# Block 0's x2 in an attention and two-MLP kernel: the last group's sum by ScalarE copies and accumulating transfers in place of VectorE adds

## The chip, the cores and the metric

The kernel runs on one core of a Trainium2 chip. The metric is the device time of one execution in microseconds (us); the median of three runs of the kernel before is 578.8 us (578.77 to 579.1). Engines are named as in the profile: PE (TensorE matmul), DVE (VectorE), ACT (ScalarE), POOL (GpSimd, which here mostly issues transfers) and SP (SyncE, which issues loads). Each engine works through its own instructions in the order in which they stand and waits for the others by semaphores.

## The reference

What is computed, cut to what matters:

```
x   = decayed linear attention of q, k, v       # batch 2, 768 steps, 8 heads of 64
xn  = x / sqrt(mean(x*x) + 1e-6) * rms_g        # 1536 tokens x 512
x2  = (silu(xn @ w_gate) * (xn @ w_val)) @ w_out   # 512 -> 1536 -> 512
h   = x2 @ w_in                                  # 512 -> 2048
out = max(0.01 * h, h) @ w_out2                  # 2048 -> 512
```

All of it is float32; the weights come as int64 bit patterns of float64 and are converted on the chip.

## The kernel before, in words

Tokens lie in three **blocks** of 512. The first MLP makes x2 from 12 slices f of 128 hidden features, in three **groups** of four (gi 0, 1, 2); the second MLP takes 16 slices in four groups (gi 3 to 6). Every float32 matmul operand is split into a **high** part (a rounded copy, by ACT) and a **low** part (the rest, by a DVE subtraction), and a product is three matmuls.

Blocks 1 and 2 are multiplied together with seven products instead of eight by `quad`: its steps p1 to p7 put half products into PSUM banks X, Y and Z. Three banks are read in mid-use: p1 fills X, ACT copies it (`kept_sum`, L1070, tile `is`), then p6 adds to X, ACT copies it again (tile `iu`), and only then may p7 add to X; DVE reads X (L1079) before p4 adds to it once more. So PE waits inside a quad for ACT's copies of bank X. Before p6 all pending entries of the list `sums` are emitted.

Block 0 is done by plain products (`whole`) and `down`. Its x2 of the three groups is summed thus: after group 0 ACT copies the four PSUM banks into the tile `more` (L752) and POOL writes them to four DRAM tiles `held` (L754); after group 1 the same with a transfer that adds in DRAM (L756); in group 2, each `down` fetches one `held` tile into a quarter of `more` (L729), and at the end `evac1` adds the four PSUM banks to the quarters with DVE (L750). After that the high parts `x2h` (ACT, L786) and low parts `x2l` (DVE, L789) of the four quarters are made; they are put on the list `sums`. The first product of the second MLP that needs them is `whole("i", f, 0)`.

The order of the work is set twice: `plan` lists PE's steps, `run` hands out conversion work and entries of `sums` between them by a planner's clocks (`spend`), and the scheduler of the tile framework then settles the place of each instruction on its engine.

Of the kernel before, what the change touches and what calls it, by code (L numbers as in the profile page):

```python
# [13 lines left out]
AF = mybir.ActivationFunctionType  # L14
ALU = mybir.AluOpType
# [6 lines left out]
G1 = [4, 4, 4]  # L22
# [4 lines left out]
SUMS = 2  # L27
# [38 lines left out]
def chain_kernel(ctx: ExitStack, tc: tile.TileContext, qk_t, kv, w1, w2, mask, qdec, kdec, sdec, rms_g, ident, out):  # L66
    nc = tc.nc
# [27 lines left out]
    held = [dram.tile([P, 512], F32, name=f"held{i}") for i in range(4)]  # L95
# [13 lines left out]
    def bank(name):  # L109
        return pools["ps"].tile([P, 512], F32, tag="bank", name=name)  # L110
# [296 lines left out]
    groups = [list(range(sum(g[:i]), sum(g[:i + 1]))) for g in (G1, G2) for i in range(len(g))]  # L407
    groups = [("gvo" if i < len(G1) else "ip", fs) for i, fs in enumerate(groups)]
# [231 lines left out]
    def need(key):  # L640
        while key not in wt:
            assert upcoming()
            convert_next()


    def product_t(dst, w, h, l, which=slice(0, 12)):

        parts = [slice(k * P, (k + 1) * P) for k in range(4)]
        pairs = [(w[:, i, part], h[:, k, :]) for k, part in enumerate(parts) for i in range(2)]
        pairs += [(w[:, 0, part], l[:, k, :] if l is not None else None) for k, part in enumerate(parts)]  # L650
        for n, (lhs, rhs) in list(enumerate(pairs))[which]:
            nc.tensor.matmul(  # L652
                out=dst, lhsT=lhs, rhs=rhs, start=(n == 0), stop=(n == len(pairs) - 1), skip_group_check=True
            )
# [5 lines left out]
    x2h, x2l = {}, {}  # L660

    sums = []
    made, parted = {}, {}
    pools = {}
    parts = {}
# [2 lines left out]
    def accumulate(L, g, f, b, start, stop, transposed):  # L668

        if start:  # L670
            acc["b"] = acc_banks(f"a{L}_{g}_{b}", 4)
        h, l = parted.pop((L, f, b))
        w = wt[f"{L}{f}"]
        for m in range(4):
            part = slice(m * P, (m + 1) * P)
            if transposed:
                terms = (w[:, 0, part], h), (w[:, 0, part], l), (w[:, 1, part], h)
            else:
                terms = (h[:, part], w[:, 0, :]), (h[:, part], w[:, 1, :]), (l[:, part], w[:, 0, :])
            cut = 256 if stop and m == 3 and g == len(groups) - 1 else 512  # L680
            for c in range(0, 512, cut):
                for n, (lhs, rhs) in enumerate(terms):
                    nc.tensor.matmul(  # L683
                        out=acc["b"][m][:, c:c + cut],
                        lhsT=lhs,
                        rhs=rhs[:, c:c + cut],
                        start=(start and n == 0),
                        stop=(stop and n == 2),
                        skip_group_check=True,
                    )  # L690
# [3 lines left out]
    def upper(key):  # L694
        if key in made:
            x = made.pop(key)
            h = gp.tile([P, 512], F32R, tag="gh", name="g{}_{}_{}h".format(*key))
            nc.scalar.activation(out=h, in_=x, func=AF.Copy)
            spend("a", 0.52)
            halves[key] = x, h  # L700

    def lower(key):
        if key in halves:
            x, h = halves.pop(key)
            l = gp.tile([P, 512], F32R, tag="gl", name="g{}_{}_{}l".format(*key))
            nc.vector.tensor_tensor(out=l, in0=x, in1=h.bitcast(F32), op=ALU.subtract)
            parted[key] = h, l
            spend("v", 0.6)
            if key[0] in "qr":
                follow(*key)  # L710
                spend("v", 0.6 if key[2] in (1, 3, 5, 6) else 0.0)
# [9 lines left out]
    def down(gi, f, b):  # L721
        kinds, fs = groups[gi]
        L = kinds[-1]
        key = (L, f, b)
        upper(key)
        lower(key)
        if gi == len(G1) - 1:
            m = f - fs[0]
            nc.gpsimd.dma_start(out=extra()[:, m, :], in_=held[m])  # L729
        accumulate(L, gi, f, b, f == fs[0], f == fs[-1], L == "o" or b > 0)  # L730
        used(f"{L}{f}")
        if f == fs[-1]:
            banks = acc.pop("b")
            first = gi in (0, len(G1))
            by_copy = gi in (0, len(G1)) or b == 0 and gi not in (len(G1) - 1, len(groups) - 1)
            later.append(("a" if by_copy else "v", 2.4, lambda: (evac1 if L == "o" else evac2)(gi, b, banks)))
        placed[0] = order.index(key) + 1

    def evac1(gi, b, banks):
        last = gi == len(G1) - 1  # L740
        if b:
            acc[b] = xp.tile([P, 4, 512], F32, tag=f"acc{b}", name=f"x2acc{b}")
            for m in range(4):
                nc.scalar.activation(out=acc[b][:, m, :], in_=banks[m], func=AF.Copy)
            return
        acc[0] = extra()
        for m in range(4):
            t = acc[0][:, m, :]
            if last:
                nc.vector.tensor_tensor(out=t, in0=banks[m], in1=t, op=ALU.add)  # L750
                continue
            nc.scalar.activation(out=t, in_=banks[m], func=AF.Copy)  # L752
            if gi == 0:
                nc.gpsimd.dma_start(out=held[m], in_=t)  # L754
            else:
                nc.gpsimd.dma_start(out=held[m], in_=t, accum_op=ALU.add)  # L756
        if last:
            high, low = x2_parts(0)
            sums.extend([lambda m=m, do=do: do(m) for do in (high, low) for m in range(4)])

    x2_ops = {}

# [17 lines left out]
    def x2_parts(b):  # L780
        if b not in x2h:
            x2h[b] = xp.tile([P, 4, 512], F32R, tag=f"xh{b}", name=f"x2h{b}")
            x2l[b] = xp.tile([P, 4, 512], F32R, tag=f"xl{b}", name=f"x2l{b}")

        def high(m):
            nc.scalar.activation(out=x2h[b][:, m, :], in_=acc[b][:, m, :], func=AF.Copy)  # L786

        def low(m):
            nc.vector.tensor_tensor(  # L789
                out=x2l[b][:, m, :], in0=acc[b][:, m, :], in1=x2h[b][:, m, :].bitcast(F32), op=ALU.subtract  # L790
            )

        return high, low
# [132 lines left out]
    def extra():  # L926
        if not more:
            more[0] = xp.tile([P, 4, 512], F32, tag="acc0", name="more")
        return more[0]
# [86 lines left out]
    def used(key):  # L1016

        n, f = key[0], int(key[1:])
        left[key] = left.get(key, 2 if doubled(n, f) else NB) - 1
        if not left[key]:  # L1020
            free(key)
# [15 lines left out]
    def consume_later(n, f, b):  # L1037
        later.append(("v" if n == "v" else "a", 0.62 if n == "v" else 0.52, lambda: consume(n, f, b)))

    def whole(n, f, b, h, l):  # L1040
        products[n, f, b] = x = bank(f"{n}{f}_{b}")
        product_t(x, wt[f"{n}{f}"], h[b], l[b])
        used(f"{n}{f}")
        consume_later(n, f, b)
# [190 lines left out]
    def pair(p):  # L1235
        return 2 * p, 2 * p + 1
# [30 lines left out]
    def do(token):  # L1267
        if token in alone:
            alone[token]()
        elif ":" in token:  # L1270
            convert_step(*token.split(":"))
        elif token[:2] in by_chunk:
            by_chunk[token[:2]](int(token[2:]))
        elif token[:2] in by_pair_of:
            by_pair_of[token[:2]](pair(int(token[2:])))
        elif token[0] == "T":
            terms.pop(token[1:])()
        else:
            n, f, b = token[1], int(token[2]), int(token[3])
            if token[0] in by_step:  # L1280
                by_step[token[0]](n, f, b)
            elif token[0] == "D":
                down(0, f, b)
            else:
                (upper if token[0] == "U" else lower)((n, f, b))
# [22 lines left out]
    def run(i, keys, b, step, behind):  # L1308
        need(keys[0])
        start = max(clock["pe"], done.get(keys[0], 0.0))  # L1310
        step()
        clock["pe"] = start + (1.36 if keys[-1] == "half" else 2.72)
        next_parts(upper)
        next_parts(lower)
        for _ in range(min(len(sums), SUMS)):
            sums.pop(0)()
            spend("v", 1.13)
            spend("a", 0.97)
        limit = clock["pe"] + (OVER if behind else 0.0)
        while upcoming():  # L1320
            key, engine, cost, _ = converting[0]
            if max(clock[engine], done.get(key, 0.0)) + cost > limit:
                break
            convert_next()
        flush()
# [73 lines left out]
```

## Time and profile before

| what | us |
|---|---|
| median of three runs | 578.8 |
| the profiled execution, its own time | 578.74 |
| its span | 576.8 |
| outside the span (578.74 - 576.8) | 1.94 |
| PE busy | 566.7 (98%) |
| DVE busy | 502.3 (87%) |
| ACT busy | 406.9 (71%) |
| POOL busy | 42.0 (7%) |

The last matmul begins at 571.84 us, and the span ends at 576.8. The place of the change lies between 315 and 345 us, where the first MLP ends and the second begins. All times within the execution are counted from the span's start.

### The profile page before, as it was taken

Reading aid. Unit: us, or ns where it says so; the run is one execution under the profiler, and the core shown is the slowest. Engines: PE = TensorE matmul, PEld = TensorE weight load, DVE = VectorE, ACT = ScalarE, POOL = GpSimd, SP = SyncE. Lnnn points to the kernel's source line nnn. Section 1 sums busy time; section 2 is a strip of 40 time slices with the busy share of each in tenths; the row PEclk is TensorE's granted clock in tenths of the full one; section 3 lists DMA queues with packets and bytes.
Section 4 is the critical chain, followed back from the end, with each engine's and each line's share of the span. In section 5 each row is a group of like instructions: output and inputs, shape, how many; then the busy total and the mean of one; then the engine's idle time right before and its main releaser. Section 6 shows DMA issues by size and latency. Waiting matters only on the chain.

```text
span 576.8 us, 8536 instructions
## 1 busy us (share of the span) xinstructions
PE 566.7 (98%) x3082; PEld 466.1 (81%) x3082; DVE 502.3 (87%) x986; ACT 406.9 (71%) x744; POOL 42.0 (7%) x49
## 2 busy tenths in 40 slices
PE   8999999999999999999999999999999999999996
PEld 5888788888888888888888878878888888888885
DVE  8899989985776899986899999999999989996792
ACT  4799768977656556977647589989868986676330
POOL 3341300010000000010000100000100020002100
PEclk9999999999999999999999999999999999999999
DMA  8991422442211122236220222224422252102455
GB/s 339 408 351 38 147 73 74 145 147 73 74 58 30 60 74 68 80 87 133 73 74 4 70 73 75 72 74 145 147 74 74 93 114 85 39 0 34 113 92 128
DMA packets 34202, 59.28 MB, mean 103 GB/s; under 512 B 19184, under 2 KB 19440, under 8 KB 34160
## 3 DMA queue, kind: packets, MB, share of 16 engines
q1 hardware_dynamic: 30864, 51.39, 26.8%
q0 software_dynamic: 3008, 7.34, 5.7%
q8 instruction: 24, 0.39, 0.3%
q14 instruction: 18, 0.15, 0.1%
q10 hardware_dynamic: 288, 0.01, 0.0%
HBM read 50.34 MB, written 8.39 MB: 102 GB/s over the span
## 4 chain that ended last, share of the span: by engine, by line
PE 87%; DVE 5%; DMA 5%; ACT 2%; issue 1%; POOL 0%; SPq 0%; DVEq 0%; POOLq 0%; ACTq 0%
PE X L853 11%; PE ao L683 9%; PE Z L853 9%; PE iX L1053 8%; PE i L652 8%; PE ap L683 7%; PE v L652 7%; PE g L652 6%; PE vX L1053 5%; PE gX L1053 5%; PE iZ L1053 4%; PE gZ L1053 2%; PE vZ L1053 2%; DMA qkv<-in_qk_t 2%; DMA qkv<-in_kv 2%; PE iY L1053 2%
## 5 line engine op out<-in xcount | busy, mean ns | idle before, releaser
L683 PE MATMUL ap<-w_p,gp_0h 128*128 128x512 f32 (+1 forms) x130 | 39.8, 386 | 0.0
L652 PE MATMUL i<-x2h,w_i 128*128 128x512 f32 x128 | 32.3, 389 | 0.0
L652 PE MATMUL g<-xh,w_g 128*128 128x512 f32 x128 | 31.8, 390 | 0.0
L652 PE MATMUL v<-xh,w_v 128*128 128x512 f32 x128 | 31.8, 390 | 0.0
L683 PE MATMUL ao<-go_0h,w_o 128*128 128x512 f32 x96 | 31.0, 389 | 0.0
L683 PEld LDWEIGHTS ap<-w_p,gp_0h 128*128 128x128 f32 x130 | 24.3, 188 | 5.0
L652 PEld LDWEIGHTS g<-xh,w_g 128*128 128x128 f32 x128 | 24.0, 188 | 5.1 <-issue 0.2
L652 PEld LDWEIGHTS i<-x2h,w_i 128*128 128x128 f32 x128 | 24.0, 188 | 5.0
L652 PEld LDWEIGHTS v<-xh,w_v 128*128 128x128 f32 x128 | 24.0, 188 | 5.0
L991 ACT ACTIVATE more<-i 128x512 f32<-128x512 f32 x16 | 9.6, 600 | 22.1 <-PE i L652 22.0
L683 PE MATMUL ap<-w_p,gp_0l 128*128 128x512 f32 (+1 forms) x65 | 25.1, 386 | 0.0
L1053 PE MATMUL iX<-th,w_si 128*128 128x512 f32 x64 | 20.7, 397 | 1.2 <-ACT iu L1070 0.7
L683 PEld LDWEIGHTS ao<-go_0h,w_o 128*128 128x128 f32 x96 | 18.0, 188 | 3.7
L1053 PE MATMUL iZ<-x2h,w_si 128*128 128x512 f32 x64 | 20.2, 391 | 0.0
L555 DVE TENSOR_TENSOR w_o<-wa_o,w_o 128x512 fp32r<-128x512 f32 x12 | 8.3, 688 | 12.5 <-ACT w_o L551 12.5
L683 PE MATMUL ao<-go_0l,w_o 128*128 128x512 f32 x48 | 18.7, 389 | 0.0
L652 PE MATMUL v<-xl,w_v 128*128 128x512 f32 x64 | 17.2, 391 | 0.0
L652 PE MATMUL g<-xl,w_g 128*128 128x512 f32 x64 | 17.2, 391 | 0.0
L884 DVE TENSOR_TENSOR y2acc<-X,y2acc 128x512 f32<-128x512 f32 x26 | 17.1, 686 | 0.2 <-PE X L853 0.2
L652 PE MATMUL i<-x2l,w_i 128*128 128x512 f32 x64 | 17.1, 389 | 0.0
L1053 PEld LDWEIGHTS iX<-th,w_si 128*128 128x128 f32 x64 | 11.8, 188 | 5.2 <-ACT iu L1070 1.4
L257 DVE TENSOR_TENSOR a<-sc,mask_sb 128x1024 f32<-128x1024 f32 (+1 forms) x13 | 14.5, 1137 | 1.1 <-PE sc L245 1.0
(372 smaller groups left out, 1824.9 us busy)
## 6 DMA issues: line engine op xcount, KB each, us to landing
raw_i<-in_w SPq DMA_DIRECT2D x16, 512.0 KB, 3.6
raw_p<-in_w SPq DMA_DIRECT2D x16, 512.0 KB, 3.6
raw_g<-in_w SPq DMA_DIRECT2D x12, 512.0 KB, 3.5
raw_v<-in_w SPq DMA_DIRECT2D x12, 512.0 KB, 3.5
raw_o<-in_w SPq DMA_DIRECT2D x12, 512.0 KB, 3.5
qkT<-in_qk_t SPq DMA_DIRECT2D x7, 512.0 KB, 8.4
kv<-in_kv SPq DMA_DIRECT2D x7, 512.0 KB, 9.2
out<-more POOLq DMA_DIRECT2D x12, 256.0 KB, 5.0
```

What stands on the lines that cost most here:

```text
L257: nc.vector.tensor_tensor(out=s["a"][:, j], in0=s["sc"][:, j], in1=mask_sb[:, j], op=ALU.mult)
L555: v.tensor_tensor(out=u[:, 1, :], in0=a, in1=u[:, 0, :].bitcast(F32), op=ALU.subtract)
L652: nc.tensor.matmul(out=dst, lhsT=lhs, rhs=rhs, start=(n == 0), stop=(n == len(pairs) - 1), skip_group_check=True)
L683: nc.tensor.matmul(out=acc["b"][m][:, c:c + cut], lhsT=lhs, rhs=rhs[:, c:c + cut], start=(start and n == 0), stop=(stop and n == 2), skip_ ...
L853: nc.tensor.matmul(out=acc[side][m], lhsT=lhs, rhs=rhs, start=(start and f == fs[0] and k == 0), stop=(f == fs[-2] and k == 2), skip_group ...
L884: nc.vector.tensor_tensor(out=dst, in0=banks[m], in1=dst, op=ALU.add)
L991: nc.scalar.activation(out=a, in_=x, func=AF.Prelu, alpha=0.01)
L1053: nc.tensor.matmul(out=dst, lhsT=lhs, rhs=rhs, start=(start and n == 0), stop=(n == 5), skip_group_check=True)
```

## The change

`evac1` no longer adds group 2's banks to a fetched sum by DVE. ACT copies each bank into its quarter of `more`, as it does for the other groups, and POOL then issues a transfer per quarter that adds the DRAM tile `held` into `more` in SBUF (`accum_op`). The four fetches in `down` go. The eight part-making operations of block 0 stand on a list of their own, `block0`; it is not emptied before p6 but when `sums` is empty or before the first `whole("i", ...)`. In the planner's clock the evacuation counts as ACT work (`by_copy`).

```diff
@@ down
         lower(key)
-        if gi == len(G1) - 1:
-            m = f - fs[0]
-            nc.gpsimd.dma_start(out=extra()[:, m, :], in_=held[m])
         accumulate(L, gi, f, b, f == fs[0], f == fs[-1], L == "o" or b > 0)
...
-            by_copy = gi in (0, len(G1)) or b == 0 and gi not in (len(G1) - 1, len(groups) - 1)
+            by_copy = gi in (0, len(G1)) or b == 0 and gi != len(groups) - 1
@@ evac1
             t = acc[0][:, m, :]
+            nc.scalar.activation(out=t, in_=banks[m], func=AF.Copy)
             if last:
-                nc.vector.tensor_tensor(out=t, in0=banks[m], in1=t, op=ALU.add)
-                continue
-            nc.scalar.activation(out=t, in_=banks[m], func=AF.Copy)
-            if gi == 0:
+                nc.gpsimd.dma_start(out=t, in_=held[m], accum_op=ALU.add)
+            elif gi == 0:
                 nc.gpsimd.dma_start(out=held[m], in_=t)
             else:
                 nc.gpsimd.dma_start(out=held[m], in_=t, accum_op=ALU.add)
         if last:
             high, low = x2_parts(0)
-            sums.extend([lambda m=m, do=do: do(m) for do in (high, low) for m in range(4)])
+            block0.extend([lambda m=m, do=do: do(m) for do in (high, low) for m in range(4)])
@@ whole
+        while n == "i" and block0:
+            block0.pop(0)()
@@ run
-        for _ in range(min(len(sums), SUMS)):
-            sums.pop(0)()
+        for _ in range(min(len(sums) + len(block0), SUMS)):
+            (sums or block0).pop(0)()
```

Three places show what the scheduler makes of it. On ACT, at the end of group 2, before: `x2h_3381<-more` are block 0's high parts, `is` and `iu` are the two copies of bank X (`iX_3396`) in the first quad of the second MLP, `wa_p` and `w_i` belong to weight conversion.

```order
L786 ACTIVATE x2h_3381<-more 128x512 [waits DVE_49] x4
L1070 ACTIVATE is_0_3407<-iX_3396 128x512 [waits PE_49]
L969 ACTIVATE th<-x2acc_1705 128x1024 [waits DVE_49]
L603 ACTIVATE wa_p_3492<-raw_p_3113 128x512 [waits DVE_49]
L991 ACTIVATE is_0_3407<-is_0_3407 128x512 [waits DVE_49]
L698 ACTIVATE gq_1h<-is_0_3407 128x512 [waits Activation_49]
L603 ACTIVATE wa_p_3534<-raw_p_3393 128x512 [waits DMAHW3_49,DVE_49]
L1070 ACTIVATE iu_0_3457<-iX_3396 128x512 [waits PE_49]
L1070 ACTIVATE is_0_3466<-iZ_3459 128x512
```

The same place on ACT in the changed kernel, from the second copy of a bank on:

```order
L747 ACTIVATE more<-ao_0_1_3305 128x512 [waits PE_49,Activation_49]
L603 ACTIVATE wa_p_3494<-raw_p_3113 128x512 [waits DVE_49]
L747 ACTIVATE more<-ao_0_2_3306 128x512 [waits PE_49,Activation_49]
L747 ACTIVATE more<-ao_0_3_3307 128x512 [waits PE_49,Activation_49]
L966 ACTIVATE th<-x2acc_1705 128x1024 [waits DVE_49]
L1069 ACTIVATE is_0_3407<-iX_3396 128x512 [waits PE_49]
L783 ACTIVATE x2h_3381<-more 128x512 [waits DMASW0_49]
L783 ACTIVATE x2h_3381<-more 128x512 [waits DMASW1_49]
L783 ACTIVATE x2h_3381<-more 128x512 [waits DMASW2_49]
L551 ACTIVATE w_i_3489<-wa_i_3433 128x512 [waits DVE_49]
L988 ACTIVATE is_0_3407<-is_0_3407 128x512 [waits DVE_49]
L783 ACTIVATE x2h_3381<-more 128x512 [waits DMASW3_49]
```

The next row there is `L1069 ACTIVATE iu_0_3451<-iX_3396 128x512 [waits PE_49]`, the second copy of bank X. The high parts now wait for the four transfers (DMASW0 to DMASW3), and the copy `iu` stands behind the fourth of them.

On PE, from the first quad's p5 on, before (`iZ_3459` is p5, `iX_3396<-th,w_si_3421` p6, `iX_3396<-th,w_si_3422` p7, `3506` and `3515` the next quad's banks):

```order
L1053 MATMUL iZ_3459<-x2h_3190,w_si_3422 128x512
L1053 MATMUL iZ_3459<-x2h_3190,w_si_3422 128x512 [waits DVE_49]
L1053 MATMUL iZ_3459<-x2l_3191,w_si_3422 128x512
L1053 MATMUL iZ_3459<-x2h_3190,w_si_3422 128x512 x2
L1053 MATMUL iZ_3459<-x2l_3191,w_si_3422 128x512
L1053 MATMUL iX_3506<-x2h_3256,w_i_3430 128x512
L1053 MATMUL iY_3515<-x2h_3256,w_i_3430 128x512 [waits DVE_49]
L1053 MATMUL iX_3396<-th,w_si_3421 128x512 [waits DVE_49]
L1053 MATMUL iX_3396<-tl,w_si_3421 128x512
L1053 MATMUL iX_3396<-th,w_si_3421 128x512 x2
L1053 MATMUL iX_3396<-tl,w_si_3421 128x512
L1053 MATMUL iX_3396<-th,w_si_3422 128x512 [waits Activation_49]
```

PE in the changed kernel, the rest of p6, p5, three matmuls of the next quad and p7's first:

```order
L1052 MATMUL iX_3396<-th,w_si_3421 128x512 [waits DVE_49]
L1052 MATMUL iX_3396<-tl,w_si_3421 128x512
L1052 MATMUL iX_3396<-th,w_si_3421 128x512 x2
L1052 MATMUL iX_3396<-tl,w_si_3421 128x512
L1052 MATMUL iZ_3453<-x2h_3190,w_si_3422 128x512 x2
L1052 MATMUL iZ_3453<-x2l_3191,w_si_3422 128x512
L1052 MATMUL iZ_3453<-x2h_3190,w_si_3422 128x512 x2
L1052 MATMUL iZ_3453<-x2l_3191,w_si_3422 128x512
L1052 MATMUL iX_3502<-x2h_3256,w_i_3430 128x512
L1052 MATMUL iX_3502<-x2h_3256,w_i_3430 128x512 [waits DVE_49]
L1052 MATMUL iX_3502<-x2l_3257,w_i_3430 128x512
L1052 MATMUL iX_3396<-th,w_si_3422 128x512 [waits Activation_49]
```

p6 now follows its first matmul at once and stands ahead of p5; p7 still waits for ACT. Since the quad begins, 26 matmuls stand ahead of p7 before the change and 27 after it.

On DVE, before, from the last low parts of block 2 on:

```order
L750 TENSOR_TENSOR more<-ao_0_0_3305,more 128x512 [waits DMASW0_49,PE_49]
L750 TENSOR_TENSOR more<-ao_0_1_3306,more 128x512 [waits DMASW1_49,PE_49]
L750 TENSOR_TENSOR more<-ao_0_2_3307,more 128x512 [waits DMASW2_49,PE_49]
L750 TENSOR_TENSOR more<-ao_0_3_3308,more 128x512 [waits DMASW3_49,PE_49]
L966 TENSOR_TENSOR x2acc_1705<-x2acc_1705,x2acc_1939 128x1024 [waits DVE_49]
L492 TENSOR_TENSOR w_si_3422<-wa_i_3108,w_si_3422 128x512
L1079 TENSOR_TENSOR is_0_3407<-iY_3409,is_0_3407 128x512 [waits PE_49,Activation_49]
L972 TENSOR_TENSOR tl<-x2acc_1705,th 128x1024 [waits Activation_49]
L492 TENSOR_TENSOR w_si_3421<-wa_i_3046,w_si_3421 128x512
L789 TENSOR_TENSOR x2l_3382<-more,x2h_3381 128x512 x4
```

The same place on DVE in the changed kernel:

```order
L492 TENSOR_TENSOR w_si_3422<-wa_i_3108,w_si_3422 128x512
L963 TENSOR_TENSOR x2acc_1705<-x2acc_1705,x2acc_1939 128x1024 [waits DVE_49]
L492 TENSOR_TENSOR w_si_3421<-wa_i_3046,w_si_3421 128x512
L555 TENSOR_TENSOR w_i_3430<-wa_i_3388,w_i_3430 128x512
L548 ISA wa_i_3433<-wa_i_3433,wb_i_3434 128x1024
L969 TENSOR_TENSOR tl<-x2acc_1705,th 128x1024 [waits Activation_49]
L1078 TENSOR_TENSOR is_0_3407<-iY_3409,is_0_3407 128x512 [waits PE_49,Activation_49]
L786 TENSOR_TENSOR x2l_3382<-more,x2h_3381 128x512 [waits DMASW0_49,Activation_49]
L786 TENSOR_TENSOR x2l_3382<-more,x2h_3381 128x512 [waits DMASW1_49,Activation_49]
L786 TENSOR_TENSOR x2l_3382<-more,x2h_3381 128x512 [waits DMASW2_49,Activation_49]
L786 TENSOR_TENSOR x2l_3382<-more,x2h_3381 128x512 [waits DMASW3_49,Activation_49]
```

The four adds are gone, the low parts of the weights (`w_si`) stand where they were, and the low parts of block 0 now wait for the transfers and for ACT. On POOL the four transfers keep their place among its instructions.

## Rows read from the trace of the kernel before

**Rows 1.** Stretches (us): each engine's busy time, its instructions, granted clock, DMA share.

```profile
core 0: us, PE busy (x) PEld busy (x) DVE busy (x) ACT busy (x) POOL busy (x), PEclk, DMA share, GB/s
329.00:338.00 9.00, 7.77 (x33) 5.83 (x32) 8.70 (x13) 7.43 (x12) 0.00 (x0) 1.00 0.18 58
338.00:572.00 234.00, 233.95 (x1031) 192.33 (x1030) 207.90 (x391) 168.44 (x298) 11.59 (x16) 1.00 0.30 82
```

**Rows 2.** Timeline of PE: start, us, instruction, idle before and its releaser.

```profile
327.43 0.61 PE L683 MATMUL ao<-go_0h,w_o 128*128 128x512 f32 x2
...
329.69 0.62 PE L1053 MATMUL iX<-x2h,w_i 128*128 128x512 f32 x2
...
332.41 0.39 PE L1053 MATMUL iX<-th,w_si 128*128 128x512 f32 x1
...
335.16 0.50 PE L1053 MATMUL iX<-th,w_si 128*128 128x512 f32 x1 [0.55 <-DVE w_si L492]
...
337.28 0.72 PE L1053 MATMUL iX<-th,w_si 128*128 128x512 f32 x2 [0.69 <-ACT iu L1070]
337.84 0.40 PE L1053 MATMUL iX<-tl,w_si 128*128 128x512 f32 x1
```

**Rows 3.** Timeline of DVE.

```profile
328.16 2.48 DVE L750 TENSOR_TENSOR more<-ao,more 128x512 f32<-128x512 f32 x4
330.56 1.22 DVE L966 TENSOR_TENSOR x2acc<-x2acc,x2acc 128x1024 f32<-128x1024 f32 x1
...
334.42 0.68 DVE L492 TENSOR_TENSOR w_si<-wa_i,w_si 128x512 fp32r<-128x512 f32 x1
```

**Rows 4.** Timeline of ACT.

```profile
314.42 1.14 ACT L786 ACTIVATE x2h<-x2acc 128x512 fp32r<-128x512 f32 x2
...
328.88 2.43 ACT L786 ACTIVATE x2h<-more 128x512 fp32r<-128x512 f32 x4 [4.75 <-DVE more L750]
...
331.81 1.06 ACT L969 ACTIVATE th<-x2acc 128x1024 fp32r<-128x1024 f32 x1
...
336.63 0.60 ACT L1070 ACTIVATE iu<-iX 128x512 f32<-128x512 f32 x1 [0.81 <-PE iX L1053]
...
468.09 0.60 ACT L918 ACTIVATE more<-ap 128x512 f32<-128x512 f32 x1 [0.18 <-PE ap L683]
```

**Rows 5.** One line: the plain fetch into SBUF, L729.

```profile
DMA to landing us min/median/max: 2.8/2.9/3.0
```

**Rows 6.** One line: the accumulating transfer of group 1, L756.

```profile
L756 POOL DMA_DIRECT2D held<-more x4: 904/1234/1430, 256.7 to 259.0; - x4
DMA to landing us min/median/max: 3.8/5.7/11.1
```

**Rows 7.** One line: the accumulating transfers of the second MLP, L922.

```profile
DMA to landing us min/median/max: 3.7/5.7/6.8
```

**Rows 8.** Timeline of POOL, in both stretches with L922.

```profile
468.99 3.65 POOL L922 DMA_DIRECT2D out<-more  x4 [56.43 <-ACT more L918]
...
471.48 1.15 POOL L922 DMA_DIRECT2D out<-more  x1
...
528.82 3.65 POOL L922 DMA_DIRECT2D out<-more  x4 [56.19 <-ACT more L918]
...
531.32 1.15 POOL L922 DMA_DIRECT2D out<-more  x1
```

**Rows 9.** DMA issues at 471.48 and at 528.82: KB, us to landing.

```profile
out<-more POOLq DMA_DIRECT2D x1, 256.0 KB, 6.1
...
out<-more POOLq DMA_DIRECT2D x1, 256.0 KB, 4.0
```

**Rows 10.** SP's timeline at 333 us, and DMA packets, 330 to 338 us.

```profile
333.45 0.33 SPq L454 DMA_DIRECT2D raw_p<-in_w  x1
...
q1 hardware_dynamic: 144, 0.52, 20.0%
```

More of the change, by code (lines that the diff above doesn't have):

```diff
@@ L662, in chain_kernel @@
     sums = []
+    block0 = []
     made, parted = {}, {}
```

## The prediction

> **What bounds the kernel now.** I read the busy times by stretch first. From 338 to 572 us PE is busy 233.95 of 234 us at a granted clock of 1.00, and from 329 to 338, where the changed instructions stand, 7.77 of 9.00 [rows 1]. So PE sets the end, and near the change it has 1.23 us of gaps; after them it has none. Whatever the change takes from or adds to PE's waits here comes through to the end unchanged, and work that it spares DVE or ACT is worth nothing by itself.
>
> PE's timeline gives the two gaps [rows 2]: 0.55 us before the matmul at 335.16, ended by DVE's low part of `w_si`, and 0.69 us before the one at 337.28, ended by ACT's second copy of bank X (`iu`). The first is p6 and the second p7 of the first quad. The gaps understate the loss, because a matmul's row is longer than its slot: from 329.69 to 332.41 PE issued 12 matmuls, 0.2267 us each [rows 2]. The 26 matmuls ahead of p7 would have taken it to 329.69 + 26 x 0.2267 = 335.58; it came at 337.28, 1.70 late.
>
> Why they were late: DVE adds the banks from 328.16 to 330.64 and only then turns to the rest; the low part of `w_si` that p6 needs runs at 334.42 [rows 3], and PE goes on at 335.16. p6 then ends late, and ACT's copy, which waited for it 0.81 us, runs at 336.63 for 0.60 [rows 4]; p7 starts 0.05 after that, at 337.28.
>
> **What the change removes.** The four adds, 2.48 us of DVE [rows 3]. With them gone, DVE can do the first `w_si` low part at 328.2, the 1.22 us subtraction, and the second low part by about 330.6, two us before p6's second matmul could start (332.41 + 0.23). That wait goes. The four fetches go too; their time was hidden, since they stood during group 2's matmuls. PE then issues without a gap up to p7: 27 matmuls now stand ahead of it, so p7 is due at 329.69 + 27 x 0.2267 = 335.81. Before, the same point of PE's work (its 28th matmul of this stretch, the second of p7) was passed at about 337.51 (337.28 + 0.23). This is the most there is to win: 337.51 - 335.81 = 1.7 us.
>
> **What it adds on ACT.** Four copies out of PSUM, 0.60 us each by the same copy of the second MLP [rows 4]. They fall into the 4.75 us in which ACT sat idle before 328.88 and just behind it [rows 4]: bank 0 is complete at 327.43 + 0.39 = 327.82 (the first of the two matmuls at 327.43 is its last [rows 2]), so copy 0 starts at about 327.9. Three more, with `wa_p` between them, end near 330.7. Then come `th` (1.06 [rows 4]) and the first copy of bank X, done at about 332.3. p6 needs it at 332.41, so there is no loss, though without that 0.1 of slack each tenth more would be a tenth on PE. Cost: nothing.
>
> **What it adds in transfers.** POOL's transfer starts 0.90 after the copy that it waits for has started (copy at 468.09 [rows 4], transfer at 468.99 [rows 8]), so the four start at about 328.8, 329.5, 330.6 and 331.1. Nothing else of POOL's is near. How long they take is the disputed cost: no accumulating transfer into SBUF is in this trace. The nearest rows:
> - Below: the plain fetch of the same bytes into the same tile lands 2.9 after its start [rows 5].
> - Between: an accumulating transfer with none ahead of it takes 3.7 to 4.0 [rows 7, 9].
> - Nearest: four accumulating transfers in a row into DRAM, issued as closely as these. In the first set of the second MLP the first lands at 468.99 + 3.7 = 472.7 and the last at 471.48 + 6.1 = 477.6; in the second at 528.82 + 4.0 = 532.8 and 531.32 + 6.8 = 538.1 [rows 7, 8, 9]. They queue: 1.63 and 1.77 us apart, the last 8.6 and 9.3 after the first was started.
> - Above: group 1's set, first start 256.7, last landing 259.0 + 11.1 = 270.1, that is 13.4 after the first start [rows 6].
>
> I take the nearest: same operation, queue and size, only the destination differs. The last of the four then lands between 328.8 + 8.6 = 337.4 and 328.8 + 9.3 = 338.1. One thing comes on top. `wa_p` now runs between the copies, so SP's next weight load, issued at 333.45 before, right after ACT has read its predecessor [rows 10], is issued near 329.8 and lies among the four. Its 144 packets hold 20.0% of 8 us [rows 10], 1.6 us of all the DMA engines. It delays the last transfer by something between 0 and 1.6; I take 0.7, which gives 338.5.
>
> **What waits for it.** ACT's order is fixed: the high parts of quarters 0 to 2, `w_i`, `is`, the high part of quarter 3, and only then `iu`, the copy for which p7 waits. With quarter 2 landing near 336.8 the first five are done by 338.4. Quarter 3's high part starts at 338.5; the next ACT instruction starts 0.51 later (two such parts in 1.14, each 0.63 [rows 4]), so `iu` runs from 339.0 to 339.6 and p7 starts 0.05 later, at 339.67. PE has waited 339.67 - 335.81 = 3.9 us there. Against the same point before: 339.67 - 337.51 = +2.2 us.
>
> Behind the waiting high part on ACT stand the copies of bank Z and the weight parts that PE needs 6 us later; behind the waiting low parts on DVE stand the low part of `w_i` and the add that frees bank X for p4. With the last low part at about 339.8 and four instructions behind it (0.6 + 3 x 0.33), that add ends near 342.1; p4 is due at 339.67 + 2.72 = 342.39. It just holds. PE's later gaps were 0.05 in all [rows 1], so nothing there pays the wait back. DVE's spared 2.4 us go into its own wait for the quarters.
>
> **The sum.** 578.74 (the profiled execution's own time) - 1.7 (both old losses) + 3.9 (the new wait) = 580.9. The median of the runs shown is 578.8, so the two may be compared directly.
>
> In general, the time is 578.74 + (L + 1.17 - 337.51), where L is the landing of the fourth transfer (0.51 + 0.60 + 0.05 = about 1.17), as long as quarter 2 lands 1.5 or more ahead of L (three ACT instructions at 0.51 stand between the two high parts). No change is then at L = 336.3.
>
> **The rivals.**
> 1. *The transfers land without queueing on each other*, 4.0 after each start: the last at 335.1. ACT then has its own chain as the limit as much as the landing; p7 starts near 337.25, the time is 578.5: no change that can be seen. For it: an SBUF destination may be quicker to read and write than DRAM. Against it: both sets in the trace queue at 1.63 to 1.77 us each, which is a rate and not a latency.
> 2. *They land like plain fetches*, 2.9 after their start, the last at 334.0, quarter 2 at 333.5. ACT's chain from there (four instructions at 0.51, then `iu`) lets p7 go at 336.15: 336.15 - 337.51 = -1.4 us, 577.4. This is the other side: the DVE relief pays, because p7's wait shrinks to 0.3. It decides once quarter 2 lands by 333.7 and the fourth by 335.2. Against it: every accumulating row is over 3.7. The Trainium skill ("DMA: Bandwidth & Descriptors", section "Anatomy of one DMA — SWDGE (gpsimd) path") gives a transfer issued by GpSimd 2.0 us plus its bytes over 436 GB/s. For these 256 KB that would be an estimate of 2.6 us by that page and a time of 577.1. The trace's plain fetches come near that rule; its accumulating transfers, at 3.7 to 11.1, do not.
> 3. *A straggler*, as in group 1's set, whose last transfer landed 11.1 after its start beside weight loads: L = 331.1 + 11.1 = 342.2, 578.74 + 5.8 = 584.6. For it: here too a load of the same size is issued among the four. Against it: one of twelve accumulating transfers.
>
> **How the numbers follow.** About 0.2% (1.16 us) is what a measurement of this kernel can tell from no change: faster below 577.6, slower above 579.9. My forecast, queueing at the rate of the rows (L from 337.5 to 341): 0.58. Straggler: 0.09. No queueing, or partly so (L from 335.1 to 337.5): 0.25, the same. Like plain: 0.08, faster. So faster 0.08, same 0.25, slower 0.67. The likeliest is 580.9; with L between 337.4 and 339.7 (no load, or all of it) its own range is 579.9 to 582.2. The range that should hold 8 in 10 leaves out the plain landing and most of the straggler: 578.2 to 583.4.
>
> **What the profile of the changed kernel would show.** Right: no gap of PE before p6; one gap of 3 to 5 us before p7's first matmul, ended by ACT `iu`; ACT idle before the high parts of quarters 1 to 3, each ended by a transfer; transfers landing from 4 to over 6 us after their start, with SP's load among them; PE without gaps after. Wrong: a landing near 3 us for all four (then the gap before p7 is under half a us); a gap at p6 (the first copy of X behind the four copies); the high part of quarter 3 no longer ahead of `iu` in time; or new gaps of PE behind 342, at p4 or in the second quad, by which DVE's and ACT's lateness would add to the sum.

## The result and the profile after

The changed kernel takes 584.26 us (median of 5 runs, 582.87 to 584.87) against 578.77 before: ratio 1.0087, 95% interval 1.0076 to 1.0099. It is slower, by 5.5 us, and lies above the range that was given. The profiled execution took 584.87 us, the longest of the five, span 583.1.

Stretches of the changed kernel, columns as in [rows 1] (the third row lies within the fourth):

```profile
core 0: us, PE busy (x) PEld busy (x) DVE busy (x) ACT busy (x) POOL busy (x), PEclk, DMA share, GB/s
329.00:338.00 9.00, 7.47 (x33) 5.82 (x31) 5.57 (x8) 4.20 (x7) 3.53 (x4) 1.00 0.64 135
338.00:344.00 6.00, 1.64 (x4) 1.35 (x5) 3.52 (x7) 4.99 (x10) 0.00 (x0) 0.63 0.33 60
344.00:346.00 2.00, 2.00 (x7) 1.52 (x6) 0.77 (x2) 1.13 (x2) 0.00 (x0) 0.50 0.00 0
344.00:350.00 6.00, 6.00 (x23) 4.79 (x22) 4.52 (x10) 4.73 (x9) 0.00 (x0) 0.80 0.26 87
350.00:572.00 222.00, 222.00 (x978) 183.13 (x978) 201.01 (x374) 162.74 (x289) 11.41 (x16) 1.00 0.30 82
```

PE stands almost still from 336 to 342, and the granted clock, 1.00 in all of [rows 1], is below 1.00 on average from 338 to 344 and from 344 to 350. From 350 on PE is full. PE's timeline:

```profile
330.13 0.61 PE L1052 MATMUL iX<-x2h,w_i 128*128 128x512 f32 x2
...
332.63 0.39 PE L1052 MATMUL iY<-x2l,w_i 128*128 128x512 f32 x1
332.86 0.63 PE L1052 MATMUL iX<-th,w_si 128*128 128x512 f32 x2
...
336.08 0.39 PE L1052 MATMUL iX<-x2l,w_i 128*128 128x512 f32 x1
342.37 1.22 PE L1052 MATMUL iX<-th,w_si 128*128 128x512 f32 x2 [5.90 <-ACT iu L1069]
343.39 0.63 PE L1052 MATMUL iX<-tl,w_si 128*128 128x512 f32 x1
343.81 1.05 PE L1052 MATMUL iX<-th,w_si 128*128 128x512 f32 x2
...
346.37 0.63 PE L1052 MATMUL iZ<-x2h,w_si 128*128 128x512 f32 x2
...
578.12 0.28 PE L684 MATMUL ap<-w_p,gp_0l 128*128 128x256 f32 x1
```

The gap before p6 [rows 2] is gone. p7 was due after 27 slots, at 330.13 + 27 x 0.2267 = 336.25, and came at 342.37: 6.12 late, in place of 1.70. Its first two matmuls take 1.22 us, before 0.72 [rows 2]. The nine matmuls from 342.37 to 346.37 took 4.00 us; at the normal slot they take 2.04.

ACT's timeline shows what held `iu`:

```profile
328.29 1.34 ACT L747 ACTIVATE more<-ao 128x512 f32<-128x512 f32 x2 [3.72 <-PE ao L684]
...
330.09 1.08 ACT L747 ACTIVATE more<-ao 128x512 f32<-128x512 f32 x2
...
332.00 0.60 ACT L1069 ACTIVATE is<-iX 128x512 f32<-128x512 f32 x1
333.18 0.63 ACT L783 ACTIVATE x2h<-more 128x512 fp32r<-128x512 f32 x1 [0.58 <-DMA more<-held]
338.38 0.63 ACT L783 ACTIVATE x2h<-more 128x512 fp32r<-128x512 f32 x1 [4.57 <-DMA more<-held]
339.64 0.63 ACT L783 ACTIVATE x2h<-more 128x512 fp32r<-128x512 f32 x1 [0.63 <-DMA more<-held]
...
341.22 0.61 ACT L783 ACTIVATE x2h<-more 128x512 fp32r<-128x512 f32 x1
341.74 0.57 ACT L1069 ACTIVATE iu<-iX 128x512 f32<-128x512 f32 x1
```

The high part of quarter 0 runs at 333.18; then ACT waits 4.57 us for the second transfer. After the third one it runs five instructions without a pause, `iu` the last, and p7 starts 0.06 after it. The transfers themselves, by their line and as issues (the load by SP's queue):

```profile
L749 POOL DMA_DIRECT2D more<-held x4: 870/952/1224, 329.2 to 331.5; - x4
...
DMA to landing us min/median/max: 4.0/8.5/9.4
```

```profile
raw_p<-in_w SPq DMA_DIRECT2D x1, 512.0 KB, 8.0
```

The first lands 4.0 after its start, at 333.2, and the last 9.4 after, at 340.9. SP's load, issued at 330.22 among them, takes 8.0 us. The four did not share the engines evenly with it: in 332 to 335 POOL's queue (q0) held 11.2% of the DMA engines' time and SP's (q1) 31.5%, in 335 to 339 POOL's held 87.8% (queue, packets, MB, share; the first two lines are 332 to 335, the last 335 to 339):

```profile
q1 hardware_dynamic: 53, 0.21, 31.5%
q0 software_dynamic: 44, 0.06, 11.2%
...
q0 software_dynamic: 330, 0.62, 87.8%
```

While the load's packets moved, POOL's queue moved almost none, though all four transfers had been issued by 332.7. From 333 to 335:

```profile
q1 hardware_dynamic: 40, 0.16, 37.1%
q0 software_dynamic: 2, 0.00, 1.1%
```

DVE's two `w_si` parts, as against [rows 3]:

```profile
328.60 0.68 DVE L492 TENSOR_TENSOR w_si<-wa_i,w_si 128x512 fp32r<-128x512 f32 x1
...
330.34 0.69 DVE L492 TENSOR_TENSOR w_si<-wa_i,w_si 128x512 fp32r<-128x512 f32 x1
```

**The sum closes.** In the profiled execution the 37th matmul of the stretch stands at 346.37, before at 339.69 (the second of the pair below): +6.68. That is the new wait 6.12, the low clock 1.96 and 0.44 by which the stretch already began late (330.13 against 329.69 [rows 2]), less 1.84 (p7's old lateness of 1.70, and 0.14 by which the nine slots behind it were longer than normal). The last matmul, at 578.12 against 571.84, is 6.28 later: 0.40 is won back behind. PE's timeline of the kernel before, at these two places:

```profile
339.46 0.62 PE L1053 MATMUL iZ<-x2h,w_si 128*128 128x512 f32 x2
...
571.84 0.28 PE L683 MATMUL ap<-w_p,gp_0l 128*128 128x256 f32 x1
```

### The profile page after: what moved, and what is told of

Its sections match the earlier page's. It is cut to its first block, busy times and chain, and to the rows that moved or that the text cites. A ratio compares the mean times of both kernels' runs of the same rounds, so it can differ in the third digit from the quotient of the medians.

```text
span 583.1 us, 8531 instructions
## 1 busy us (share of the span) xinstructions
PE 568.6 (98%) x3082; PEld 468.0 (80%) x3082; DVE 502.0 (86%) x982; ACT 408.1 (70%) x748; POOL 43.1 (7%) x49
## 4 chain that ended last, share of the span: by engine, by line
PE 45%; issue 35%; DMA 8%; DVE 6%; ACT 5%; POOL 1%; DVEq 0%; POOLq 0%; ACTq 0%
PE ap L684 7%; PE X L850 7%; PE i L652 7%; PE iX L1052 7%; PE Z L850 6%; PE iZ L1052 4%; PE v L652 2%; DMA raw_v<-in_w 2%; PE iY L1052 2%; PE g L652 2%; DMA qkv<-in_kv 2%; DMA more<-held 1%; DMA kv<-in_kv 1%; PE ao L684 1%; DVE xg L387 1%
```

## The experiments

Theory L: the load among the four transfers makes them late, ACT's fixed order carries the lateness to `iu` and p7, and PE's lower clock behind the wait is added. Rival S: accumulating transfers into SBUF are this slow by themselves. (Some expectations say theory Q: the transfers' own low rate, carried through ACT's order.) Each profile shows one execution of several; where it lies far from the median, this is said. Edits are against the changed kernel unless said.

**1. Without the load.**

```diff
@@ fetch
+            if key == "p2":
+                raw[key] = raw["p1"]
+                return
```

> The changed kernel, but the weight load that SP issues beside the four accumulating transfers is left out (one weight slice, p2, is computed from p1's data); ACT's order around the high parts is the same. Theory L (the load beside them is what stretched the transfers): the second to fourth land like the sets in the trace of before, the last 8.6 to 9.3 us after the first start instead of 11.7, the third near 336.7 instead of 339.6; PE's wait before p7 falls from 5.9 to 3.0 to 3.5 us and the time to 580.5 to 582. Theory S (accumulating into SBUF beside it is slow by itself): landings, wait and time stay as in the changed kernel, 583 to 585.

584.19 us, 1.0088 (1.0073 to 1.0103). It tells nothing on the load: SP issued the next one in its place, into `raw_i` at 330.20, and the transfers were late again (the last 10.4 after the first start, PE's wait 4.62).

**2. Plain transfers in place of accumulating ones.**

```diff
-                nc.gpsimd.dma_start(out=t, in_=held[m], accum_op=ALU.add)
+                nc.gpsimd.dma_start(out=t, in_=held[m])
```

> The changed kernel, but the four transfers copy the held sum into the tile instead of adding it (group 2's own part of block 0's x2 is lost); same bytes, same waits, same order on ACT, load beside them kept. Theory Q (the accumulation's low rate is the cost, and everything that waits does so through ACT's queue): the transfers land 3 to 4 us after their start, PE's wait before p7 is under 0.5 us, and the time is 577.2 to 577.8, faster than before. Rival (any POOL transfer beside the load is late, or the clock or order loses elsewhere): 579 to 584.

580.27 us, 1.0027 (1.001 to 1.0044): theory Q's 577.2 to 577.8 was missed, the rival's 579 to 584 held. Its ten runs spread from 578.48 to 583.11, and the profiled one took 582.74, the second longest. Its transfers and PE's wait:

```profile
DMA to landing us min/median/max: 2.9/6.1/6.3
```

```profile
339.65 1.22 PE L1052 MATMUL iX<-th,w_si 128*128 128x512 f32 x2 [3.53 <-ACT iu L1069]
```

The first lands in 2.9 as [rows 5], the other three, with the load among them, in 6. So it is not the addition alone. Plain transfers did share the engines with the load: from 333 to 334 POOL's queue held 38.0% and SP's 52.4%.

**3. The parts only where they are used.** `block0` is emptied in `whole` alone, so three of the four high parts stand behind `iu` on ACT.

```diff
@@ run
-        for _ in range(min(len(sums) + len(block0), SUMS)):
-            (sums or block0).pop(0)()
+        for _ in range(min(len(sums), SUMS)):
+            sums.pop(0)()
```

> The changed kernel, with block 0's parts handed out only just before the first product that uses them, so that only one of the four high parts stands ahead of the copy iu on ACT. Theory Q: PE's wait before p7 is under 0.6 us; the other three high parts now stand ahead of the second quad's copies, and PE waits there 1.5 to 3 us instead; the time is 579 to 581. Rival (the transfers hurt in another way than through ACT's queue): 583 to 585.

578.35 us, 0.9995 (0.9985 to 1.0004), better than expected. No wait before p7; one in the second quad, and the clock stays:

```profile
343.54 0.72 PE L1052 MATMUL iX<-th,w_si 128*128 128x512 f32 x2 [1.08 <-ACT is L1069]
```

The transfers took up to 8.2 us here too. What cost 5.5 us is the place in ACT's queue from which they were waited for.

**4. The list alone.** The kernel before, its eight parts put on `block0` as in the change; banks, adds and fetches as before.

> The kernel before (VectorE adds, fetches in down), with only the second edit: block 0's parts on the list block0. The order around the first quad is the same as before on ACT, DVE and PE. Theory Q (the loss is all in copies and transfers): no change, 578.4 to 579.2. Rival (the later making of the parts costs or gains by itself): over 579.9 or under 577.6.

578.92 us, 1.0002 (0.9993 to 1.0011): the list does nothing, and the two old gaps (0.55 and 0.69) are there.

**5 and 6. The load made to wait** for quarter 3's high and low part, by a small DVE operation that reads both the raw weights and the low part; 6 with plain transfers.

```diff
+    tiny = xp.tile([P, 1], F32, name="tiny")
@@ prepare
+            if key == "p0":
+                nc.vector.tensor_tensor(
+                    out=tiny, in0=high[:, :1].bitcast(F32), in1=x2l[0][:, 3, :1].bitcast(F32), op=ALU.max
+                )
```

> The changed kernel, all of its work kept, but SP's weight load that lay among the four transfers is held back until block 0's last low part is made (one DVE instruction of a single column reads the load's buffer and that low part); ACT's order is the same. Theory L (the load beside them stretched the second to fourth transfer): they land 1.6 to 1.8 us apart behind the first, the last 8.6 to 9.3 us after the first start, PE's wait before p7 is 2.8 to 3.4 us, the time 580.5 to 582.5. Theory S (accumulating into SBUF is slow by itself): wait 4.5 to 6 us as in the changed kernel, 583 to 585.

> As the run with the load held back, and the four transfers copy instead of adding (group 2's own part of block 0's x2 is lost). Theory L with Q: with neither the addition nor the load, each lands about 2.9 us after its start, PE waits under 0.6 us before p7, the clock stays at 1.00, the time is 577.2 to 578. Rival (a transfer behind ACT's copies is late whatever it does): a wait of 2 us or more and 580 or more.

594.85 us (1.0277) and 591.73 (1.022), far above all expectations and inconclusive as times. With the tile of 4 bytes PE's slots were longer from 100 us on (experiment 5, 380 to 420 us):

```profile
380.00:420.00 40.00, 40.00 (x172) 31.94 (x171) 38.54 (x76) 36.64 (x67) 0.00 (x0) 1.00 0.32 105
```

172 matmuls where the changed kernel issues 178. Near the change PE waited 2.71 (5) and 1.25 (6), and in 5 the last transfer landed 8.7 after the first start. Experiments 9 and 10 repeat them with a tile of 256 bytes.

**7. A fill for the wait.** 24 spare matmuls into a bank of their own ahead of p7.

```diff
@@ p7
+            if n == "i" and f == 0:
+                spare = acc_bank(0, "spare")
+                for k in range(24):
+                    nc.tensor.matmul(
+                        out=spare, lhsT=wt[own[0]][:, 0, :P], rhs=x2h[1][:, 0, :], start=True, stop=True
+                    )
```

> The changed kernel with 24 more matmuls on PE just ahead of p7, on data that has long been there, into a bank that nothing reads: some 5.4 us of PE work in the wait. Theory C (part of the loss is TensorE's lower granted clock after the wait): p7 starts when it did, 4.5 to 6 us late, but the granted clock stays at 1.00 behind it, and the time is about 2 us under the changed kernel's, 581 to 583. Rival (the slow matmuls behind the wait have another cause, or the wait alone makes the loss): 584 to 586.

588.91 us, 1.0168, outside both expectations. The time is spoilt: DVE's and ACT's order moved too, and another wait came up before p4. But PE's rows tell of the clock:

```profile
335.30 5.60 PE L1109 MATMUL spare<-x2h,w_i 128*128 128x512 f32 x24
341.18 0.73 PE L1052 MATMUL iX<-th,w_si 128*128 128x512 f32 x2 [0.28 <-ACT iu L1069]
...
348.78 1.22 PE L1052 MATMUL iX<-th,w_i 128*128 128x512 f32 x2 [4.57 <-DVE is L1078]
```

With PE kept busy, p7 goes at the normal pace (0.73); behind the idle 4.57 us further on the pair takes 1.22 again.

**8. The adds late.** The kernel before with DVE's four adds and the eight parts on `block0`, emptied only in `whole`.

```diff
-                nc.vector.tensor_tensor(out=t, in0=banks[m], in1=t, op=ALU.add)
+                block0.append(lambda t=t, m=m: nc.vector.tensor_tensor(out=t, in0=banks[m], in1=t, op=ALU.add))
```

> The kernel before with the sum left on VectorE (no copies by ACT, no accumulating transfers), but the four adds and the parts handed out just before the first product that uses them. Theory Q (the 1.7 us of PE's two old waits come from the adds standing ahead of the weight part on DVE): both waits go, 577.0 to 578.0, faster than both kernels. Rival (the adds only move the wait to the second quad): 578.4 to 580.

577.9 us, 0.9986 (0.9976 to 0.9996). Both old gaps are gone without any new transfer (two stretches):

```profile
329.00:338.00 9.00, 9.00 (x41) 7.38 (x41) 9.00 (x17) 7.70 (x14) 0.00 (x0) 1.00 0.29 90
338.00:344.00 6.00, 6.00 (x28) 4.95 (x27) 5.62 (x11) 6.00 (x12) 0.00 (x0) 1.00 0.12 40
```

**9. The load behind the transfers, with the tile of 256 bytes.** As 5, with `xp.tile([P, 64], ...)` and its first column written.

> The run with the load behind the transfers again, with a small tile of 256 bytes per partition in place of 4 bytes, so that the tiles behind it keep their alignment to 256 bytes. If the 2.7% of that run came from the tile alone, PE's issue slot in 380 to 420 us is 0.2267 us again here. Theory L (the load among the four sets the landings): the four transfers start at 329.2 to 331.5, the third lands near 336.5 to 337.5 and the fourth near 338 to 339; PE waits 2.3 to 3.4 before p7, the clock falls in part or not at all, time 580.5 to 582.5. Theory S (the accumulating transfers are that slow by themselves): third and fourth land at 339.5 to 341 as with the load, PE waits 5 to 6, time 583 to 585.

582.14 us, 1.0049 (1.0031 to 1.0066), as theory L had it. The transfers; ACT's waits; PE:

```profile
DMA to landing us min/median/max: 4.2/6.4/7.3
```

```profile
335.95 0.63 ACT L789 ACTIVATE x2h<-more 128x512 fp32r<-128x512 f32 x1 [2.20 <-DMA more<-held]
337.23 0.63 ACT L789 ACTIVATE x2h<-more 128x512 fp32r<-128x512 f32 x1 [0.65 <-DMA more<-held]
```

```profile
339.95 1.22 PE L1058 MATMUL iX<-th,w_si 128*128 128x512 f32 x2 [3.79 <-ACT iu L1075]
```

The third lands at 337.2 and the last at 331.2 + 7.3 = 338.5, 9.6 after the first start; with the load it was 340.9 - 329.2 = 11.7. Between these two profiles the load cost 2.1 us. In the other profiles with a load among four accumulating transfers the last landed 10.4 (1), 10.5 (3, 11), 10.8 (7) and 11.7 (12) after the first start, so the cost against 9 is 0.8 to 2.1. PE's wait was above the 3.4 expected, and the clock fell here too.

**10. The same with plain transfers.**

> The same with plain transfers instead of accumulating ones (group 2's part of block 0's x2 is lost). Theory L: without the load the four plain transfers land 2.9 to 4.5 after their start, PE waits at most 1.3 before p7, the clock stays at 1.00, time 577.2 to 578.6. Theory S for plain transfers (POOL's transfers into a tile that ACT has just written are slow whatever lies beside them): landings of 6 as with the load, wait 3 to 4, time 580 to 581.5.

578.52 us, 0.9988 (0.9977 to 1.0). The transfers and PE:

```profile
DMA to landing us min/median/max: 2.9/3.2/3.4
```

```profile
336.72 0.73 PE L1058 MATMUL iX<-th,w_si 128*128 128x512 f32 x2 [0.60 <-ACT iu L1075]
```

Between the two profiles the landings fall from 6 us to 3.2 with the load gone, and the wait from 3.53 to 0.60. But 2's profile was the second longest of its ten runs, and this one, at 577.51, the shortest of its ten; the medians, 580.27 and 578.52, lie 1.75 apart. 9 and 10 together: the load and the addition each make the landings late, and S alone is refuted.

**11. The parts on the old list.** The changed kernel with `sums.extend` in place of `block0.extend`.

> The changed kernel with the eight parts of block 0 on the old list in place of the list of their own. The order of ACT, DVE and PE from 328 to 345 us is the same but for the numbers of buffers, so the list of its own should be worth nothing here: 583 to 585, with the wait of 5 to 6 before p7 and the lower clock behind it. Against it: if the list matters by a way not seen in the order, 580 or less.

584.26 us, 1.0084 (1.0065 to 1.0104): the same as the changed kernel. Its profile, at 584.48, gives a second look at the same order: the stretch began 1.14 later (331.27), but the last transfer landed 10.5 after the first start, and p7 came at 342.34 after a wait of 4.79. POOL's queue stood still here too while the load moved, and the load was faster (334 to 336):

```profile
q1 hardware_dynamic: 88, 0.36, 90.0%
q0 software_dynamic: 2, 0.00, 0.1%
```

**12. Transfers kept, parts and first plain products later**, at the end of the second quad.

```diff
@@ the steps of a quad
-                        if i7 in BEHIND[2] and own:
+                        while (i7 == 6 if first else i7 in BEHIND[2]) and own:
...
+                            if not first:
+                                break
@@ run: as in 3
```

> The changed kernel with the parts of block 0 taken off run's hands (made only before the plain product that needs them) and these plain products themselves put later, to the end of the second quad. No transfer is waited for ahead of the copy that p7 needs nor ahead of the next quad's copies. Theory (ACT's queue holds the copies back): no wait of PE over 0.3 us between 329 and 350, clock 1.00, time 577.0 to 578.2, as the run with late adds. Rival: the transfers' load on the DMA engines costs elsewhere (weights come late), then 578.5 to 580.

577.64 us, 0.9976 (0.9964 to 0.9987), the fastest of all, though its interval meets that of 8. Its profiled execution took 579.49, the slowest of its 12 runs; one wait of 1.18 stands in the second quad, at 345.24, against the expectation. Its transfers are as late as the changed kernel's, yet PE runs through up to 344 at full clock (line; two stretches):

```profile
DMA to landing us min/median/max: 4.0/8.2/9.4
```

```profile
329.00:338.00 9.00, 8.92 (x40) 7.06 (x39) 9.00 (x17) 8.46 (x16) 3.52 (x4) 1.00 0.67 119
338.00:344.00 6.00, 6.00 (x27) 4.67 (x25) 4.39 (x9) 4.71 (x9) 0.00 (x0) 1.00 0.68 171
```

## Why the prediction was right and wrong

**Right: what bounds, what is won, and by what it is lost.** PE's waits came through to the end, since PE is full from 350 on. The two old losses went: both `w_si` parts ran within 0.5 us of the times forecast. ACT's four copies were hidden, and p6 went without a gap. The new wait stands where it was put, before p7, ended by `iu`, held behind the high parts, though at 5.90 us it is above the 3 to 5 forecast. 3 shows the cause by moving only those parts; 12, which moves the first plain products too, agrees. "PE without gaps after" held.

**Wrong: the size of the landing, "which gives 338.5".** The fourth transfer landed at 340.9, 2.4 later. Of this 0.4 is the first start (329.18 for 328.8). About 0.6 is the queueing of the four, which was nearly right: without the load the last lands 9.6 after the first start (experiment 9), where the rows gave 8.6 to 9.3. The other 1.4 is the term on top. I gave the load "something between 0 and 1.6" and took 0.7, its share of the DMA engines' time; against 9 it cost 2.1 in this profile and 0.8 to 2.1 over the six with a load among the four. So 0.7 was too small against 9 each time. Whether 1.6 is a bound is not settled: two of the six profiles are above it, four below, and without the load 5 had the last landing at 8.7 and 9 at 9.6.

Even sharing was the wrong picture, too. POOL's queue stood nearly still while most of the load moved (1.1% from 333 to 335 here, 0.1% from 334 to 336 in 11), and the load itself held 37.1% of the engines' time in the one and 90.0% in the other. The cost goes with the load's own time to landing: 2.1 where the load took 8.0 us (here) or 6.5 (12), 0.8 to 1.2 where it took 5.5 to 6.0 (1, 3, 7 and 11). The Trainium skill ("DMA: Bandwidth & Descriptors", section "Issuing engines are not separate DMA queues") says that transfers of all issuing engines run on the same 16 DMA engines and interleave; the later landings agree with the first, but in these stretches the accumulating transfers hardly interleaved with the load (2 packets to 40, and 2 to 88). Why they stood still, and why the load was slow here, stays open.

**Wrong in the formula: which landing counts.** It took the fourth, "as long as quarter 2 lands 1.5 or more ahead". It landed about 1.3 ahead (339.6 and 340.9), so ACT's chain from the third set `iu`. p7 came at 342.37 instead of 339.67, 2.70 later; of this 0.44 was already there at 330.

**Missing: the clock.** I added the wait and nothing for what follows it. The nine matmuls behind it ran mostly at the lower of the two levels (1.2 GHz; granted 0.50 from 344 to 346), and cost 1.96. With that, 2.70 + 1.96 = 4.66 against a miss of 584.87 - 580.9 = 3.97; the rest is the 0.40 won back, the 0.14 of longer slots and 0.17 less time outside the span (584.87 - 583.1 against 1.94). That idleness brings the lower clock is shown by 7, and the other kernels agree: the pair behind a gap took 0.72 or 0.73 us where that gap was 0.60 (10), 0.69 (before), 1.08 (3) or 1.18 (12), and 1.22 where it was 3.53 (2), 3.79 (9), 4.57 (7), 4.62 (1) or 5.90. Two lie between: 0.88 behind 2.71 (5, with its longer slots) and 1.03 behind 4.79 (11). In 9 the nine matmuls to 343.51 took 3.56 us, 1.5 too long. The Trainium skill ("TensorE: Matmul & The Clock Gate", Part 1) says that an idle TensorE falls back to the lower clock and that activity releases it; the trace agrees, with 0.50 granted from 344 to 346 behind the idle 5.90 us and 1.00 from 350 on.

**A slip in the sum.** By the prediction's own formula L from 337.4 to 339.7 gives 579.8 to 582.1; it has 579.9 to 582.2. Nothing hangs on it.

**The rivals.** "No queueing" fell by 9. "Like plain fetches" fell by its own rule: even plain transfers took 6 us beside the load (2), and accumulating ones without it 4.2 to 7.3 (9). Plain ones without the load took 2.9 to 3.4 (10). The Trainium skill ("DMA: Bandwidth & Descriptors", section "Anatomy of one DMA — SWDGE (gpsimd) path") gives 2.0 us plus the bytes over 436 GB/s, an estimate of 2.6 us for these 256 KB; 10 comes near it. The straggler's time, 584.6, came nearest, in part by luck: its reason, a load among the four, was half right, but three of the four were late and not one, and a third of what was lost was the clock, which it did not have.

**What the change would need.** The transfers do no harm if nothing urgent stands behind the waits: 12 keeps them and wins 1.3 us. But 8 wins 0.9 with no transfer at all, by moving block 0's adds and parts away from p6 and p7. What the transfers add to that is not shown: the intervals of 8 and 12 meet, and 12 moves plain products too.

## What to carry to other kernels

Before a transfer is put ahead of something urgent, look at what other loads are issued in the same microseconds: beside one load of 512 KB these four landed 0.8 to 2.1 us later, where 0.7 was allowed for. On an engine that works in order, put what waits for a transfer behind the copies that PE needs next; the same late transfers cost 5.5 us in one order and nothing in another. And price a long wait of PE above its length: behind those of 3.8 and 5.9 us here, 1.5 and 2.0 us came on top.

## What the runs showed that was not expected

**A 4-byte tile cost 2.2%.** Experiment 5 took 594.85 us and 9, which differs in that tile alone, 582.14. In 5 the matmul slots were longer from 100 us on: 40 us held 172 matmuls. With 256 bytes (9) they held 177:

```profile
380.00:420.00 40.00, 40.00 (x177) 32.78 (x176) 39.10 (x78) 36.71 (x67) 2.21 (x4) 1.00 0.35 118
```

That the small tile shifted the tiles allocated behind it, and that their alignment is the cause, is argued from the two sizes and not shown.

**A like stretching sits beside group 1's transfers**, and varies from profile to profile. There a weight load lands late, and ACT waits for it at 267 us; in the kernel before 1.08 us, in the changed kernel 1.73, in experiment 12 2.90 (ACT's timeline of the three):

```profile
266.65 0.67 ACT L604 ACTIVATE wb_i<-raw_i 128x512 int32<-128x512 uint32 x1 [1.08 <-DMA raw_i<-in_w]
```

```profile
267.23 0.66 ACT L604 ACTIVATE wb_i<-raw_i 128x512 int32<-128x512 uint32 x1 [1.73 <-DMA raw_i<-in_w]
```

```profile
268.35 0.67 ACT L604 ACTIVATE wb_i<-raw_i 128x512 int32<-128x512 uint32 x1 [2.90 <-DMA raw_i<-in_w]
```

PE then waited 0, 0.21 and 1.37 us ten us later. Over all profiles PE did not wait where ACT waited up to 1.45, and above that PE waited about 1.5 less than ACT, in experiment 6, with its longer slots, 2.2 less. That the transfers beside it make the load late is argued, not shown. It fits that 12's profiled run lies 1.9 us above its median; for runs without a profile it is only argued.
